# Anew ordering the 1,099 steps of a convolution-and-FFN kernel: other 32-row runs, other places for loads

## The chip, the cores and the metric

One core of a Trainium2 chip runs the whole kernel. The metric is device time in microseconds (us) of one execution. The core has a matrix engine (PE, whose weight loads appear apart as PEld), a vector engine (DVE), a scalar engine for activations (ACT), a fourth engine called POOL, and SP, which does nothing here but issue transfers. Transfers move data between DRAM and the on-chip memory SBUF, 128 partitions wide. PE writes its results into eight banks of a second on-chip memory, PSUM; DVE or ACT must empty a bank before PE can use it again.

## The reference: what is computed

Two branches work on the same layernormed input `xn` (2048 rows, 640 columns, bf16), and are multiplied together:

```python
kv  = shift_conv(k, shift_k) * v                        # 4 taps along the rows
y   = irfft(rfft(kv) * rfft(ssm_k))[:2048] + kv * ssm_D # a convolution as long as the sequence
s   = xn * y
g   = silu(gelu(xn @ w1 + b1) @ w2 + b2)                # FFN, 640 -> 1728 -> 640
out = x + s * g
```

## The kernel before

**The FFN branch.** The rows are worked in four chunks of 512. For a chunk, `xn` is transposed on PE (step `tt`, L488) and copied out of PSUM (`te`); fourteen groups `h` of five matmuls each (L504, the last and narrower one L500) make the hidden layer, each followed by a gelu on ACT (`he`, L516 and L513); eight groups `g` of fourteen matmuls of 320 columns (L537) make the output, each with a silu on ACT (`ge`, L545) and a multiply into `xn` (`gm`, L553) on DVE (suffix `.d`) or POOL (`.p`). The last chunk adds the input on DVE (`ga`, L561) and stores from SP (`gs`, L572).

**The convolution branch** computes Fourier transforms as matmuls in two stages. First the taps run on DVE (`cv`, L630 to L641), and the filter is transposed (`kt` L577, copied by `kc`). First stage: `kf` and `uf` (L588, evacuated by `ke` and `ue`), whose results go to DRAM scratch by POOL's stores (`ks` L603, `us` L614) and come back in another layout by SP's loads (`fl` L646 for the filter, `ml` L694 for the data). Second stage: `ff` and `mu` (L451), products with the filter (`mp`, `mq` on DVE, L717; some inputs are first copied by ACT, `mv`, L711) and the first stage of the inverse, `ma` and `mb` (L451). Here `fe` evacuates `ff`, `me` evacuates the inverse, and `mk` (L700, two loads) makes a copy of the filter's transform with neighbouring partitions swapped. POOL stores (`ms`, L744), SP loads back (`yl`, L751), the second inverse stage `y` runs on PE (L759 and L760), DVE multiplies by `xn` (`yt`, L768), adds the input (`yo`, L773) and POOL stores (`ys`, L777). Evacuations are a copy or cast on ACT (suffix `.a`, L145) or DVE (`.d`, L146).

**The 32-row calls.** The second stage works on blocks of 32 rows. One call of `blocks` issues four matmuls of 32x32 weights by 512 columns:

```python
def blocks(out, m, rhs, turn, form, start=True, stop=True):
    t = int(TURNS[turn])
    ...
    for i in range(P // QB):
        j = (i + t) % (P // QB)
        a, b = (slice(x * QB, (x + 1) * QB) for x in ((i, j) if m == F2 else (j, i)))
        nc.tensor.matmul(out=out[b, :], lhsT=mats[a, m, a], rhs=rhs[a, :], start=start, stop=stop)
```

The digit of `TURNS` for the call's number shifts the four blocks: with turn t, rows i of the array meet columns i+t (forward `ff`, `mu`) or rows i+t meet columns i (inverse `ma`, `mb`). So the sixteen 32x32 tiles of PE's array are used four by four, and two neighbouring calls use the same tile where their turns put them there. There are 160 calls, 640 such matmuls; calls that follow each other on PE without other work between form what is called a run below.

**What sets the order.** A string `PLAN` lists all steps after a fixed opening (`prologue`): a kind, a number and, where there is a choice, an engine or form as a suffix. `steps` (L925 and following) maps a kind to a function. The steps are issued in that order; each engine keeps its own instructions in this order, SP its loads, POOL its stores. PSUM banks and the SBUF slots are handed out by free lists in the same order, so who waits for whose buffer follows from the string too. The first loads of the string are `X` (input chunks, L275), `C` (filter, L305, 512 KB each), `K` (L280 to L282, 640 KB), `V` (L285, 320 KB) and `B` (second FFN weights, L309; the last with two small ones, L311 and L312). Small steps in it: `ls`, `lv`, `lr`, `lb`, `ln` are the layernorm (L458 to L481; `lr` is POOL's power, L467, `lb` is L471), `ir` five POOL instructions (L657 to L660), `s` two on DVE (L417, L418), `q` loads of the input (L748).

Of the kernel before, what the change touches and what calls it, by code (L numbers as in the profile page):

```python
# [38 lines left out]
ke13.a kc12.d gm1.d kf37 kc3.a kf5 kt13 X3 kt15 kc7.d kf3 kf30 ke37.a kf4 kc2.d kf23 ke12.a K1 kc13.d kf31 ke3.a ke4.a
d kt11 kt6 gm0.d kc15.d kt8 ke31.a ke30.d kc11.a kt9 kc6.d kc8.d kc9.a ke5.d kt14 kc14.d kt5 kf34 V1 ke23.a kf35 kf18  # L40
K2 V6 kf26 kc5.d kt0 ke34.a kf14 ke26.a kc0.d ke14.a kf33 kf38 kf45 ke45.a kf43 ke43.a g3 V4 kf15 ke35.a kf36 cv6 ks1
ke33.a kf2 V2 kf22 ke18.a ge3 kf1 ke38.a ke2.a ks11 kf0 ke1.a cv16 kf21 ke0.a g5 ke15.d ke22.a V0 kf44 ke36.a ir ke21.a
cv17 kf46 ge5 gm3.d kf10 ke10.a kf32 kf16 kf17 ke44.a ks12 cv18 ke16.a ks0 kf19 ke32.a cv7 ke19.a ke46.a g7 kf9 kf7
ke17.a ge7 ks10 kf20 ke20.a ks6 kf11 cv19 kf41 cv20 ke7.a kf47 ks4 gm5.d ke47.a kf27 kf28 ks7 g6 ke27.a ks15 uf1 kf40
kf29 ke11.a cv21 ke28.a cv8 kf8 ke9.a ke41.a kf39 ke40.a ke8.a ke39.a ks13 ue1.d uf2 V7 uf7 g4 ke29.a ue2.a ks5 ks9 kf6
X2 ge6 uf4 ge4 cv22 ue7.a kf24 ke6.a V5 kf25 uf9 kf42 h24 uf3 V3 cv23 uf8 ke42.a ke25.a uf0 cv9 ue9.a ke24.a uf6 ue4.a
ue6.a ue8.a cv24 ks3 ue3.a gm7.d h17 ks14 uf5 cv10 uf28 ue5.a cv11 uf11 ue11.a h14 ks2 ue0.a ls9 uf27 h19 h20 he14 ks8
ue27.a uf31 h16 ue31.a ue28.a h18 us2 he17 he19 he24 uf10 h22 ue10.a he16 he22 uf26 uf29 uf30 uf34 ue34.a h23 uf35 h15
# [10 lines left out]
fe30.a fe12.a mk5 ff3.f g11 ff15.q ff16.q ls12 ff17.q fe3.a fe36.d fe33.a ge11 tt10 fe15.d fe16.a ff1.q fe17.a lv3 lr3
mu8.q ff4.q te10.d mu9.f gm11.p fe4.a ff20.q mu7.f mu5.f mq9 fe1.d mv8 mq7 h30 ml5 mv5 h31 h34 mk4 mp9 mu6.q fl15 lb3  # L60
ff25.f ml0 mp5 mp8 mu11.q he30 fe20.d mk1 mu12.q he31 ma9.f ff22.q mp7 mq5 mb9.f mq6 he34 h38 mu10.f fe25.a mv11 me9.a
mp6 ff21.q mk0 fe22.a ma7.f ff37.q fe21.a gm10.p ln12.d mp12 mp10 mb7.f he38 mq10 mu14.q ln13.d mv14 mp11 me7.a fe37.a
h35 h33 ma5.q mu1.q mq12 ln14.d mb5.f ml6 mu0.f he35 ma10.f mu13.q mq1 he33 ff38.q fe38.a me5.a ma6.f mb6.f ml1 mp14
mp1 ml8 mp0 mb10.q h41 me10.a ml12 he41 me6.a h28 mq0 h36 mu3.f he28 ff39.q ml13 mu20.q mu2.q he36 mu4.f mp13 h32 mq13
mk6 ff31.f mk8 mv20 mq3 mk13 mp3 ma3.f mq14 mv2 ma0.f mu15.f fe39.a ml9 mu32.f mb3.f mb0.f ml10 mk9 he32 me0.a mq4
fe31.a mk12 me3.a h29 mp2 h37 mk7 mq15 h39 mv32 ma2.q mq11 he29 mu33.f ma14.q q6 ma12.f mp4 he37 he39 mq2 mb14.q mp15
mp32 mu23.f mq8 mb2.f mb12.f ml15 h40 mp20 mv23 ml14 me2.a mq33 mp33 mu30.q ln15.d me12.a mp23 me14.a mu21.q ma1.q
ma8.q ma11.q mq21 mb1.q mb8.q mb11.q tt16 te16.d mk10 he40 me1.a g17 tt15 mp21 mq20 mu31.q me8.a mp30 mu22.q mq30
mu26.q mp22 ge17 tt19 me11.a ml11 mq31 g18 mp31 te19.a mv26 mu34.q ma31.f te15.a mq22 mq23 ma20.q ma30.q ge18 gm9.p
mp26 ma13.q mb31.f ml7 me31.a q5 ma23.q gm17.p mu25.q mb13.q me13.a mb30.f mp34 mb23.f mq26 me23.a q1 mb20.q me20.a  # L70
mk14 mp25 tt17 g22 mq34 te17.a ma22.q ma32.f mk11 mq32 mu18.q mu16.f ma21.q me30.a mb22.q mb32.q mq25 mb21.q ge22
me21.a me22.a mu17.f q3 mv17 g16 mp18 mq16 me32.a ms3 mu24.q mp16 mq18 ge16 ma4.q gm16.p mu19.q mp17 ma26.q ma34.q
mb4.q mq24 mp19 ma25.q mb34.q ma33.f mb26.q me26.a mp24 me34.a mb25.f me25.a g19 ma24.q mu27.q me4.a mq19 mb24.q mu29.q
# [10 lines left out]
ga26 ys0 g28 yo4.d yt17 yo5.d gs27 ge28 yt22 yt23 gm28.d g25 gm29.d ys5 ge30 ga28 ga29 ge25 gm30.d gm25.d ga25 gs29 g31
ga30 ge31 gm31.d gs25 ys4 gs30 gs31
"""


# [868 lines left out]
```

## Time and profile before

| what | value |
| --- | --- |
| time, median of 3 | 190.81 us (190.59 to 191.03) |
| the profiled execution's own time | 190.82 us |
| its span in the profile | 189.0 us |
| granted PE clock | 0.996 |
| PE busy | 182.8 us, 97% |
| DVE busy | 166.6 us, 88% |
| ACT busy | 158.5 us, 84% |
| POOL busy | 62.3 us, 33% |
| bytes moved | 57.67 MB, mean 305 GB/s |

A row of a timeline has the start and the length in us, the engine, the line of the kernel, the operation, what is written and read, the shape, the number of instructions put together, and in brackets the idle time before them with what ended it. Neighbouring matmuls overlap, so a stretch's length on PE is read from its first start to the start of what follows, and not from the sum of its instructions.

### The profile page before, as it was taken

Reading aid. Unit: us, or ns where it says so; the run is one execution under the profiler, and the core shown is the slowest. Engines: PE = TensorE matmul, PEld = TensorE weight load, DVE = VectorE, ACT = ScalarE, POOL = GpSimd, SP = SyncE. Lnnn points to the kernel's source line nnn. Section 1 sums busy time; section 2 is a strip of 40 time slices with the busy share of each in tenths; the row PEclk is TensorE's granted clock in tenths of the full one; section 3 lists DMA queues with packets and bytes.
Section 4 is the critical chain, followed back from the end, with each engine's and each line's share of the span. In section 5 each row is a group of like instructions: output and inputs, shape, how many; then the busy total and the mean of one; then the engine's idle time right before and its main releaser. Section 6 shows DMA issues by size and latency. Waiting matters only on the chain.

```text
span 189.0 us, 4812 instructions
## 1 busy us (share of the span) xinstructions
PE 182.8 (97%) x1808; PEld 110.2 (58%) x1808; DVE 166.6 (88%) x317; ACT 158.5 (84%) x309; POOL 62.3 (33%) x98
## 2 busy tenths in 40 slices
PE   6899999999999999999999999999999999999992
PEld 2486468977764455665653344465645544677671
DVE  7979899999999999999999999999999600489993
ACT  3757999899999999999999999999898989952021
POOL 8545200029845104157216000030596620010320
PEclk9999999999999999999999999999999999999998
DMA  5999999959899899989789999699799869992545
GB/s 188 376 370 314 347 398 410 358 166 395 329 361 364 287 321 381 297 337 350 236 263 278 341 316 328 229 360 332 234 342 326 317 201 300 394 399 94 212 160 188
DMA packets 26399, 57.67 MB, mean 305 GB/s; under 512 B 3016, under 2 KB 14857, under 8 KB 26376
## 3 DMA queue, kind: packets, MB, share of 16 engines
q1 hardware_dynamic: 21872, 39.65, 61.1%
q0 software_dynamic: 4320, 17.70, 25.4%
q8 instruction: 14, 0.23, 0.5%
q14 instruction: 9, 0.07, 0.1%
q10 hardware_dynamic: 184, 0.01, 0.1%
HBM read 33.76 MB, written 18.35 MB: 276 GB/s over the span
## 4 chain that ended last, share of the span: by engine, by line
PE 85%; DVE 5%; DMA 4%; ACT 3%; issue 1%; SPq 0%; DVEq 0%
PE banks L537 31%; PE banks L504 24%; PE banks L588 9%; PE banks L451 7%; DMA w_sb<-in_B_w_dram 4%; PE banks L832 4%; PE banks L577 3%; PE banks L759 2%; PE banks L760 2%; DVE area L146 2%; PE banks L488 1%; ACT area L145 1%; DVE area L717 1%; PE banks L500 1%; DVE st L458 1%
## 5 line engine op out<-in xcount | busy, mean ns | idle before, releaser
L145 ACT CAST area<-banks 128x512 bf16<-128x512 f32 (+2 forms) x153 | 74.5, 592 | 2.8 <-PE banks L451 1.8
L537 PE MATMUL banks<-w_sb,hT 128*128 128x320 bf16 (+1 forms) x462 | 65.7, 295 | 0.0
L537 PEld LDWEIGHTS <-hT 128*128 128x128 bf16 x462 | 43.7, 98 | 18.1 <-issue 1.9
L504 PE MATMUL banks<-xnT,w_sb 128*128 128x512 bf16 x230 | 53.3, 379 | 0.1
L504 PEld LDWEIGHTS <-w_sb 128*128 128x128 bf16 x230 | 21.7, 98 | 26.7 <-issue 3.5
L516 ACT ACTIVATE hT<-banks,b_f 128x512 bf16<-128x512 f32 x52 | 32.7, 707 | 2.8 <-PE banks L832 1.7
L717 DVE TENSOR_TENSOR area<-banks,area 128x512 bf16<-128x512 f32 x54 | 34.6, 686 | 0.1
L545 ACT ACTIVATE sl<-banks 128x320 bf16<-128x320 f32 (+1 forms) x33 | 14.6, 451 | 14.8 <-PE banks L537 12.9
L553 POOL TENSOR_TENSOR xn<-xn,sl 128x320 bf16<-128x320 bf16 x13 | 10.6, 827 | 48.9 <-ACT sl L545 26.0
L641 DVE TENSOR_TENSOR area<-area 128x2560 bf16<-128x2560 bf16 x16 | 23.5, 1485 | 0.6 <-DMA area<-in_A_k_dram 0.5
L768 DVE TENSOR_TENSOR area<-banks,xn 128x426 bf16<-128x426 f32 (+1 forms) x18 | 10.0, 596 | 14.0 <-PE banks L760 14.0
L451 PE MATMUL banks<-area,mats 32*32 32x512 bf16 x640 | 18.8, 380 | 0.6 <-DVE area L146 0.5
L637 DVE TENSOR_TENSOR area<-area 128x2560 bf16<-128x2560 bf16 x12 | 17.9, 1492 | 0.2
L603 POOL DMA_DIRECT2D scrK<-area x16 | 8.9, 560 | 24.3 <-DVE area L146 18.4
L588 PE MATMUL banks<-area,WB 128*128 128x426 bf16 (+1 forms) x64 | 15.5, 299 | 0.0
L614 POOL DMA_DIRECT2D scrU<-area x16 | 8.7, 547 | 20.6 <-ACT area L145 20.6
L588 PE MATMUL banks<-area,WA 128*128 128x428 bf16 (+1 forms) x64 | 15.4, 298 | 0.0
L146 DVE CAST area<-banks 128x512 bf16<-128x512 f32 (+2 forms) x23 | 14.2, 638 | 0.3 <-ACT area L145 0.2
L451 PEld LDWEIGHTS <-mats 32*32 32x32 bf16 x640 | 6.7, 88 | 10.7 <-issue 8.9
L744 POOL DMA_DIRECT2D scrC<-area x16 | 11.7, 734 | 3.0 <-ACT WB L674 1.4
L717 DVE TENSOR_TENSOR area<-area 128x512 bf16<-128x512 bf16 x26 | 10.5, 420 | 0.0
L458 DVE BATCH_NORM_STATS2 st<-xn 128x6 f32<-128x320 bf16 x24 | 10.4, 476 | 0.0
(109 smaller groups left out, 218.6 us busy)
## 6 DMA issues: line engine op xcount, KB each, us to landing
scrK<-area POOLq DMA_DIRECT2D x16, 320.0 KB, 4.1
scrU<-area POOLq DMA_DIRECT2D x16, 320.0 KB, 3.6
...
```

The lines of the kernel that those rows point to most:

```text
L145: return nc.scalar.copy(out=out_ap, in_=in_ap)
L146: return nc.vector.tensor_copy(out=out_ap, in_=in_ap)
L451: nc.tensor.matmul(out=out[b, :], lhsT=mats[a, m, a], rhs=rhs[a, :], start=start, stop=stop)
L458: nc.vector.bn_stats(out=st[:, j, h, :], in_=xn_tiles[c][:, j, h * HALF:(h + 1) * HALF])
L504: nc.tensor.matmul(out=ps, lhsT=w1_sb[:, t, ft * P:(ft + 1) * P], rhs=xnT[:, t, :], start=(t == 0), stop=(t == DT - 1))
L516: nc.scalar.activation(out=hT[:, ft, :], in_=one(("h", i)), func=ACT.Gelu_apprx_tanh, bias=b1_f[:, ft:ft + 1], scale=1.0)
L537: nc.tensor.matmul(out=ps[:, 0:ws.stop - ws.start], lhsT=hT[0:M, ft, q * P:(q + 1) * P], rhs=w2_sb[0:M, ft, hs.start + ws.start:hs.start + ...
L545: nc.scalar.activation(out=sl[:, ws], in_=one(key)[:, 0:ws.stop - ws.start], func=ACT.Silu)
L588: nc.tensor.matmul(out=ps[:, dst], lhsT=(WA, WB)[r][:, n2, :], rhs=rows[:, n2 % 2, src], start=True, stop=True)
L637: nc.vector.tensor_tensor(out=uc, in0=uc, in1=tmp, op=ALU.add)
L641: nc.vector.tensor_tensor(out=tmp if s else uc, in0=kh[:, r0:r0 + KR, :].rearrange("p (a b) d -> p a b d", a=2), in1=w_exp[:, j:j + 1, Non ...
L717: nc.vector.tensor_tensor(out=p_part(i, x), in0=u, in1=span(name, i), op=ALU.mult)
```

## The change

Two constants change and nothing else: `TURNS` and `PLAN`. The number of steps of each kind and the opening are kept; so is the number of matmuls and of transfers. What moves is the order, and with it some suffixes: filter copies `kc` on DVE 12 to 14, transposes `te` on DVE 10 to 9, `fe` on DVE 11 to 9, `ue` on DVE 8 to 7, `me` on DVE 1 to 3, `ln` on DVE 11 to 12, `gm` on DVE 19 to 20 (each of these goes to or comes from ACT, those of `gm` POOL).

```diff
-TURNS = "303222211332100321313102031211323202233020231231"
+TURNS = "333223311110212303012132122202110030313111121121"
 PLAN = """
-he2 w X1 ls5 h12 h13 h10 C1 ws1 he12 he4 ls6 h9 ls7 he0 he5 ls4 s he10 he9 K0 lv1 B0 lr1 cv1 lb1 ln7.d ln4.d ln6.d he13
...
```

Both orders divide the 160 calls into 22 runs. Calls in each run, in the order of the program:

```
before  2 7 4 6 8 3 7 7 6 10 5 7 8 8 3 12 9 11 6 12 11 8
after   2 7 6 4 3 6 5 6 11 6 10 6 7 3 9 12 9 10 7 13 10 8
```

How often the most used tile of the array is used within each run, worked out from `TURNS` and the order:

```
before  1 2 1 2 4 1 2 3 4 4 2 3 2 3 1 4 3 3 2 5 4 2   sum 58
after   1 2 2 1 1 2 2 3 5 2 5 2 2 1 3 4 3 3 2 4 3 2   sum 55
```

**SP, the loads of the opening.** Before, all of the second FFN weights (L309, L311, L312) stand ahead of the second to fifth filter load (L305):

```order
L305 DMA area<-in_A_ssm_k_dram 128x2048
L280 DMA area<-in_A_k_dram 112x1920
L281 DMA area<-in_A_k_dram 15x1920
L282 DMA area<-in_A_k_dram 128x2560
L309 DMA w_sb<-in_B_w_dram 128x5x640 x2
L309 DMA w_sb<-in_B_w_dram 128x3x640
L311 DMA w_sb<-in_B_w_dram 64x640
L312 DMA w_sb<-in_B_b_dram 1x640
L305 DMA area<-in_A_ssm_k_dram 128x2048 x4
```

The same place on SP in the changed kernel:

```order
L282 DMA area<-in_A_k_dram 128x2560
L309 DMA w_sb<-in_B_w_dram 128x5x640
L305 DMA area<-in_A_ssm_k_dram 128x2048
L309 DMA w_sb<-in_B_w_dram 128x5x640
L309 DMA w_sb<-in_B_w_dram 128x3x640
L311 DMA w_sb<-in_B_w_dram 64x640
L312 DMA w_sb<-in_B_b_dram 1x640
L305 DMA area<-in_A_ssm_k_dram 128x2048 x3
```

One filter load of 512 KB now stands ahead of two of the three large weight loads and the two small ones.

**DVE, the second chunk's layernorm and first transposes** (L641 and L637 are taps and a product of the convolution, L481 the layernorm of a quarter chunk, L146 COPY xnT the first copies of transposes). Before:

```order
L418 TENSOR_SCALAR area<-area 128x384
L463 TENSOR_SCALAR ve_340<-mv_289 128x4
L641 TENSOR_TENSOR area<-area 128x2560
L471 SCALAR_TENSOR_TENSOR nb_346<-mv_289,rs_343 128x4
L481 TENSOR_SCALAR xn<-xn,mv_289,rs_343 128x640 x4
L641 TENSOR_TENSOR area<-area 128x2560
L637 TENSOR_TENSOR area<-area 128x2560
L146 COPY xnT<-banks 128x512
```

In the changed kernel:

```order
L463 TENSOR_SCALAR ve_348<-mv_324 128x4
L641 TENSOR_TENSOR area<-area 128x2560 x2
L417 TENSOR_SCALAR area<-area 128x384
L418 TENSOR_SCALAR area<-area 128x384
L471 SCALAR_TENSOR_TENSOR nb_372<-mv_324,rs_370 128x4
L481 TENSOR_SCALAR xn<-xn,mv_324,rs_370 128x640 x4
L637 TENSOR_TENSOR area<-area 128x2560
L146 COPY xnT<-banks 128x512 x2
```

Two taps and the steps L417 and L418 now stand between L463 and the four L481, where one tap stood before. On POOL the five instructions of `ir`, which stood behind the first two stores of scratch, now stand ahead of the second chunk's L467.

**DVE, the products of the second stage.** L717 are the products, with `banks` where they read PSUM; L146 CAST 128x512 the evacuation of `ff`. Before, from the first product on:

```order
L717 TENSOR_TENSOR area<-banks,area 128x512
L146 CAST area<-banks 128x512
L717 TENSOR_TENSOR area<-banks,area 128x512 x2
L471 SCALAR_TENSOR_TENSOR nb_1480<-mv_1179,rs_1422 128x4
L717 TENSOR_TENSOR area<-area 128x512 x2
L146 CAST area<-banks 128x512
L717 TENSOR_TENSOR area<-banks,area 128x512
L717 TENSOR_TENSOR area<-area 128x512
L717 TENSOR_TENSOR area<-banks,area 128x512 x2
L481 TENSOR_SCALAR xn<-xn,mv_1179,rs_1422 128x640
```

In the changed kernel, from the first product on:

```order
L717 TENSOR_TENSOR area<-banks,area 128x512 x2
L146 CAST area<-banks 128x2x256
L717 TENSOR_TENSOR area<-banks,area 128x512 x3
L471 SCALAR_TENSOR_TENSOR nb_1507<-mv_1216,rs_1505 128x4
L717 TENSOR_TENSOR area<-area 128x512
L717 TENSOR_TENSOR area<-banks,area 128x512
L717 TENSOR_TENSOR area<-area 128x512
L717 TENSOR_TENSOR area<-banks,area 128x512 x4
L481 TENSOR_SCALAR xn<-xn,mv_1216,rs_1505 128x640
L717 TENSOR_TENSOR area<-banks,area 128x512 x7
```

The two evacuations of `ff` that DVE did among its products are one, and it stands ahead of L471; `ff` evacuations behind it are ACT's.

**SP, the reloads of the same stage** (L694 `ml`, L700 `mk`, L748 `q`). Before, from the last filter reload on:

```order
L646 DMA area<-scrK 128x2x640
L694 DMA area<-scrU 128x2x640
L700 DMA area<-area 64x1280 x4
L694 DMA area<-scrU 128x2x640 x5
L700 DMA area<-area 64x1280 x6
L694 DMA area<-scrU 128x2x640 x2
L700 DMA area<-area 64x1280 x6
L748 DMA area<-in_A_q_dram 128x1280
```

In the changed kernel, to the same place (the first L748):

```order
L694 DMA area<-scrU 128x2x640 x2
L700 DMA area<-area 64x1280 x2
L694 DMA area<-scrU 128x2x640 x2
L700 DMA area<-area 64x1280 x4
L694 DMA area<-scrU 128x2x640
L700 DMA area<-area 64x1280 x2
L694 DMA area<-scrU 128x2x640
L700 DMA area<-area 64x1280 x2
L694 DMA area<-scrU 128x2x640
L700 DMA area<-area 64x1280 x2
L748 DMA area<-in_A_q_dram 128x1280
```

The five data reloads that stood together are divided: swapped copies (L700) stand between them, each of which waits until the evacuations that it copies are done. In steps: `ml12 mk6 ml8 ml6 mk10 mk11 ml9 mk8 ml11 mk9 ml10 mk12 q5`, where it was `ml0 mk1 mk0 ml6 ml1 ml8 ml12 ml13 mk6 mk8 mk13 ml9 ml10 mk9 mk12 mk7 q6`. The data reload `ml6` feeds `mu15`, `ml8` feeds `mu20`, and `ml10` feeds `mu26`.

**DVE, the end.** L553 are the last multiplies by the silu, L561 the additions of the input (the last two of each work on 160 columns). Before:

```order
L773 TENSOR_TENSOR area<-area 128x1280
L768 TENSOR_TENSOR xn<-banks,xn 128x426 x2
L553 TENSOR_TENSOR xn<-xn,sl_2731 128x320
L553 TENSOR_TENSOR xn<-xn,sl_2706 128x320
L561 TENSOR_TENSOR xn<-xn,area 128x320 x2
L553 TENSOR_TENSOR xn<-xn,sl_2752 128x320
L553 TENSOR_TENSOR xn<-xn,sl_2756 128x320
L561 TENSOR_TENSOR xn<-xn,area 128x320 x2
L553 TENSOR_TENSOR xn<-xn,sl_2791 128x160
```

In the changed kernel:

```order
L553 TENSOR_TENSOR xn<-xn,sl_2743 128x320
L768 TENSOR_TENSOR area<-banks,xn 128x426
L773 TENSOR_TENSOR area<-area 128x1280
L553 TENSOR_TENSOR xn<-xn,sl_2746 128x320
L553 TENSOR_TENSOR xn<-xn,sl_2750 128x320
L561 TENSOR_TENSOR xn<-xn,area 128x320 x3
L553 TENSOR_TENSOR xn<-xn,sl_2784 128x160
```

A multiply by `xn` (L768) and an addition of 1280 columns (L773) stand nearer to the end, and three L561 in a row stand ahead of the last L553.

More of the change, by code (lines that the diff above doesn't have):

```diff
@@ L39 @@
[L39 to L48, printed above, removed]
@@ L59 @@
[L59 to L68, printed above, removed]
@@ L69 @@
[L69 to L73, printed above, removed]
@@ L84 @@
[L84 to L85 removed]
+he2 X1 C1 w ir h8 he1 h10 he5 K0 B1 ws1 he10 h6 h7 he3 ls7 he0 h13 ls4 ls5 ls6 lv1 C3 h9 B0 cv0 h11 B2 he4 cv1 s lr1
+lb1 he13 ln6.d ln5.d ln4.d ln7.d he8 C0 h12 tt6 he9 tt7 he11 cv2 he6 tt5 te6.d te7.d tt9 tt8 cv3 he7 C2 he12 te5.a
+te9.d ss g0 g1 te8.d ge0 g3 cv4 C4 kt7 gm0.d kt15 sm kt4 cv5 ws0 ws2 d kc7.d kc15.d ge1 V7 ge3 kc4.d kt0 kc0.d kt8 kt9
@@ new lines @@
+uf45 ue38.d uf43 uf46 ls9 uf39 ue36.a us10 g8 ff20.q ue45.a ff35.q ue44.a ue39.d us13 ue43.a ue47.a ue46.a ff5.f us15
+us14 us12 ff7.f gm11.d ls10 ff0.q lv2 ge8 fe35.a ff8.q ff25.f fl1 fe8.a fe5.a g13 ff4.q fe20.a fe7.d lr2 fe0.d ff9.f
+ff11.q ls12 lb2 ln8.d fe25.a ff22.q ff31.q fe9.a gm10.p fe31.a fe4.a ge13 mk3 ff12.f fl13 fe22.a ln11.d fe12.a g9
+ff30.f ge9 ff6.f fe6.a ff28.q ff23.q fl6 fe23.a ls13 gm8.d g14 fe30.a ln10.d ln9.d ml3 fe11.a tt10 tt14 ls15 fe28.d
+tt12 tt13 te10.d ml2 ff2.q ge14 ml5 ff14.q ff10.q tt11 te14.d mk2 ff24.q te12.a fe10.a ff21.f te13.d ff32.q fe2.d
@@ new lines @@
+ff26.q ff18.q te11.d ff34.q g15 ls14 fe14.a mk5 fe21.d fe24.d ff27.f fe26.a gm14.p ff17.f fe32.a fe34.a ml4 fe18.a
+ff3.f ge15 mk4 lv3 gm15.p ff1.f mu9.q h34 h32 he34 fe27.d ff16.q mu14.f ml0 mu5.q fe3.d mu7.q mp9 mq9 fe1.a fe17.d he32
+ff38.f mu6.f h37 fe16.a mq7 h29 ml13 mu8.f mp7 mk0 mk1 ff29.q mv5 mq6 lr3 lb3 mv14 ff15.q mp5 he37 fe38.a he29 ml1 mp6
+mu10.f mq5 mu11.q ma7.f mp10 fe29.a ma5.f mv11 mv8 mu13.q mq10 mb5.q mu12.f mq12 mp12 ml12 fe15.a mb7.f me5.a me7.a
+ln12.d mk6 h40 he40 ma12.q mu0.q mb12.f ml8 mu1.f ff33.q me12.a ff19.q ml6 fe19.a h28 mq13 mk10 he28 h38 mp13 mq0 mp1
@@ new lines @@
+fe33.a ma6.f mk11 mu2.f mu4.f ma10.q mp0 gm9.p he38 mb6.f ma9.q mb9.f mq1 mq4 ln13.d me6.a mp14 ff37.q fe37.a ln15.d
+ln14.d ml9 mp8 mk8 me9.a mb10.f ff39.q mp4 h41 he41 h36 h30 ma0.q mq14 mu32.q mu15.f mq8 mp15 mp11 me10.a fe39.a mu20.f
+mq11 mv2 he36 mb0.f mv20 mp20 mp2 mu3.q mv32 mq3 ml11 mk9 h31 h33 me0.a h39 he31 mp3 ma4.f he30 mu24.f ma13.f mu16.q
+he33 mb4.f ml10 mb13.q ma2.q tt16 mq15 h35 mk12 ms2 he39 gm13.p mq2 mu23.q me4.a mq16 mb2.f q5 me13.a mk13 te16.a he35
+ml7 mp16 mu22.q tt15 g19 ma14.q mq20 mp24 ma11.q me2.a te15.d mk15 mp22 ma8.q mu30.f ml15 mv23 mq24 mu26.q mb14.f mq22
@@ L86 @@
+g30 ga26 yt2 yt23 g28 ge30 gs25 ge28 gm27.d ga27 ge29 gs27 yo0.d gm30.d yt4 g31 ge31 yo1.d gm28.d gm29.d ys0 ys1 ga30
+gs30 ga29 ga28 gs29 gm31.d gs31
 """
```

52 lines of the change are left out of this document (30 added, 22 removed).

## Prediction

> **What bounds the kernel now.** I read the page first: the share of each engine and the chain of waits.
>
> ```profile
> span 189.0 us, 4812 instructions
> PE 182.8 (97%) x1808; PEld 110.2 (58%) x1808; DVE 166.6 (88%) x317; ACT 158.5 (84%) x309; POOL 62.3 (33%) x98
> PE 85%; DVE 5%; DMA 4%; ACT 3%; issue 1%; SPq 0%; DVEq 0%
> ```
>
> PE sets the end: 85% of the chain is its own work, and no matmul is added or removed. An order can only change what PE loses between matmuls. So I read the PE timeline from 76 to 147 us, where the 32-row runs lie. Pieces of it:
>
> ```profile
> 91.74 0.62 PE L451 MATMUL banks<-area,mats 32*32 32x512 bf16 x24
> 92.30 2.08 PE L537 MATMUL banks<-w_sb,hT 128*128 128x320 bf16 x14
> ...
> 98.46 0.42 PE L451 MATMUL banks<-area,mats 32*32 32x512 bf16 x12
> 98.81 0.40 PE L488 MATMUL banks<-ident,xn 128*128 128x128 bf16 x4
> 99.14 0.70 PE L451 MATMUL banks<-area,mats 32*32 32x512 bf16 x16
> 100.01 0.53 PE L451 MATMUL banks<-area,mats 32*32 32x512 bf16 x12 [0.17 <-DVE area L146]
> 100.47 3.41 PE L504 MATMUL banks<-xnT,w_sb 128*128 128x512 bf16 x15
> 103.81 0.61 PE L451 MATMUL banks<-area,mats 32*32 32x512 bf16 x16
> 104.75 0.61 PE L451 MATMUL banks<-area,mats 32*32 32x512 bf16 x12 [0.33 <-DVE area L146]
> ...
> 106.52 1.04 PE L451 MATMUL banks<-area,mats 32*32 32x512 bf16 x24
> 107.50 2.33 PE L504 MATMUL banks<-xnT,w_sb 128*128 128x512 bf16 x10
> ```
>
> Two runs have 24 matmuls, or 6 calls, each. The first takes 92.30 - 91.74 = 0.56 us from its first start to the next work, the second 107.50 - 106.52 = 0.98. In the first the busiest 32x32 tile is used twice, in the second four times. The run of 12 matmuls at 98.46 uses each tile once and takes 98.81 - 98.46 = 0.35. So a run costs about 0.35 plus (0.56 - 0.35) = 0.21 for each further use of one tile ((0.98 - 0.56) / 2 = 0.21 too). What a run costs above that is a wait: at 99.14 the run of 28 (a tile used twice) takes 1.33 instead of 0.56, at 103.81 it takes 1.54 (four times, 0.98 expected). The first start of the second half is late in both, and both name a cast on DVE (L146).
>
> The same reading over all 22 runs gives 18.3 us, against 16.2 if none waited; some 2.1 us are waits. I made both sums from the timeline's L451 rows and their followers; the first is at 77.48, the last at 145.81:
>
> ```profile
> 77.48 0.41 PE L451 MATMUL banks<-area,mats 32*32 32x512 bf16 x8
> ...
> 145.81 0.65 PE L451 MATMUL banks<-area,mats 32*32 32x512 bf16 x32
> ```
>
> **The runs.** Both orders have 22 runs, so what it costs to enter and leave 32-row work is paid as often. The uses of the busiest tile, added over the runs, fall from 58 to 55: 3 x 0.21 = 0.6 us less. The best case is 0.65 and the worst nothing, if it is not the tile that sets a run's length.
>
> Here the Trainium skill ("TensorE: Matmul & The Clock Gate", section "Measured speedup vs the span model") would give another answer: it makes the span of packed tiles one matmul plus about 4 ns for each further tile, which counts tiles and not their repeats. By it the term would be zero. The trace does not agree: two runs of 24 matmuls take 0.56 and 0.98 us. But one of them may hide a wait without a record, so I keep this as a rival.
>
> **The opening.** DVE's and PE's timelines of before:
>
> ```profile
> 19.33 0.17 DVE L463 TENSOR_SCALAR ve<-mv 128x4 f32<-128x4 f32 x1
> 20.03 1.49 DVE L641 TENSOR_TENSOR area<-area 128x2560 bf16<-128x2560 bf16 x1 [0.54 <-DMA area<-in_A_k_dram]
> 21.44 0.15 DVE L471 SCALAR_TENSOR_TENSOR nb<-mv,rs 128x4 f32<-128x4 f32 x1
> 21.52 1.51 DVE L481 TENSOR_SCALAR xn<-xn,mv,rs 128x640 bf16<-128x640 bf16 x4
> ...
> 24.79 0.83 PE L488 MATMUL banks<-ident,xn 128*128 128x128 bf16 x12
> 25.46 3.97 PE L537 MATMUL banks<-w_sb,hT 128*128 128x320 bf16 x28
> ```
>
> Before, DVE waits for a load until 20.03, does one tap, and has the four L481 done at 21.52 + 1.51 = 23.03, well before PE's first L488. Now a second tap (21.44 - 20.03 = 1.41 from start to start) and L417 and L418 come ahead of L471; the two stood inside that wait before:
>
> ```profile
> 18.71 0.31 DVE L417 TENSOR_SCALAR area<-area 128x384 int32<-128x384 f32 x1
> ...
> 19.58 1.05 POOL L467 TENSOR_TENSOR rs<-ve,mhalf 128x4 f32<-128x4 f32 x1 [2.73 <-DVE ve L463]
> 42.59 0.16 POOL L657 IOTA kcol<- 128x1 f32 x1
> ...
> 45.27 2.40 POOL L660 TENSOR_SCALAR kj<-kj,kcol 128x16 int16<-128x16 int16 x1
> ```
>
> L417 and L418 take 19.33 - 18.71 = 0.62. The last L481 ends at 23.03 + 1.41 + 0.62 = 25.06. PE has the same eight `h` groups ahead of its first L488, so its turn comes at 24.8 again; a transpose step takes the four normalised pieces one after another, so only its last waits: 0.1 to 0.4 us. POOL's five `ir` instructions, 45.27 + 2.40 - 42.59 = 5.1 us, now stand ahead of the power (L467) that L471 needs. POOL was free from 19.58 - 2.73 = 16.85, so the power ends at 16.85 + 5.1 + 1.05 = 23.0, and DVE reaches L471 at 21.44 + 1.41 + 0.62 = 23.5. The taps hide it, by 0.5; without them L471 and all behind it would be later by what is missing.
>
> The second FFN weights come next. L311 is the last of them but one (the last row, L312, is 1.2 KB):
>
> ```profile
> 16.94 1.62 SPq L311 DMA_DIRECT2D w_sb<-in_B_w_dram  x1
> DMA to landing us min/median/max: 9.6/9.6/9.6
> DMA packets 2616, 5.69 MB, mean 379 GB/s; under 512 B 162, under 2 KB 1820, under 8 KB 2614
> ```
>
> Before it landed at 16.94 + 9.6 = 26.5, and the first L537 group needed it for its fourteenth matmul. Now 512 KB go ahead, at the 379 GB/s of the stretch from 17 to 32 us 1.4 us: 27.9. But all five transpose steps now stand ahead of that group: it begins at 24.8 + 20 x 0.06 = 26.0 (12 transposes took 25.46 - 24.79 = 0.67), its eleventh to fourteenth matmul run 10 to 13 x 0.138 later, 27.4 to 27.8 (28 matmuls of 320 take 3.97). That loses 0 to 0.4, and less where the transposes were late themselves. I take +0.3 for the opening; bounds 0 and +0.9.
>
> **The waits in the runs.** The two recorded waits come from DVE's casts of `ff` among the products:
>
> ```profile
> 102.67 0.76 DVE L471 SCALAR_TENSOR_TENSOR nb<-mv,rs 128x4 f32<-128x4 f32 x1
> ...
> 104.02 0.68 DVE L146 CAST area<-banks 128x512 bf16<-128x512 f32 x1
> ```
>
> The cast at 104.02 stands behind an L471 of 0.76 us, and the call at 104.75 needs the bank that it empties at 104.70. In the new order DVE's last cast of `ff` stands ahead of L471; the `ff` evacuations behind it are ACT's. So 0.17 + 0.33 = 0.5 us go. What is late next: the banks that the products themselves empty, since DVE stays full (10.00 of 10.00 us):
>
> ```profile
> 100.00:110.00 10.00, 9.66 (x116) 3.82 (x118) 10.00 (x21) 9.60 (x18) 3.29 (x4) 1.00 0.99 314
> L146 DVE COPY area<-banks 128x640 bf16<-128x640 bf16 x12 | 5.4, 485 | 0.4 <-ACT area L145 0.2
> L145 ACT COPY area<-banks 128x640 bf16<-128x640 bf16 x4 | 2.8, 702 | 0.2 <-PE banks L577 0.2
> ```
>
> (Behind the colon: length, then busy us of PE, PEld, DVE, ACT and POOL, the clock, the DMA share, GB/s.) Of the moved suffixes only the two `kc` weigh: +2 x 0.485 = 1.0 us on DVE, -2 x 0.70 = 1.4 on ACT, both long before this stage; the others nearly cancel (`fe` -2 against `me` +2). So I see no relief for DVE beyond the 0.5, and take -0.5. The bounds are -2.1 (all waits go) and +1.6 (rival 1).
>
> **The tail.** PE's work from the first `y` on is the same. DVE's end of before:
>
> ```profile
> 182.19 1.10 DVE L768 TENSOR_TENSOR xn<-banks,xn 128x426 bf16<-128x426 f32 x2
> ...
> 185.21 0.24 DVE L553 TENSOR_TENSOR xn<-xn,sl 128x160 bf16<-128x160 bf16 x1
> ...
> 186.05 0.24 DVE L561 TENSOR_TENSOR xn<-xn,area 128x160 bf16<-128x160 bf16 x1
> ```
>
> From the L768 to the last pieces DVE has 185.21 - 182.19 = 3.0 us of work in a row. In the new order its last multiplies wait for the last silus but one, and behind them stand three L561 of about 0.24 before the last pieces; the last matmuls and the last silu are where they were. That fits in by a hair: +0.1, bounds 0 and +0.3 (one L561).
>
> **The sum**, against the profiled execution's own 190.82 (the median of three is 190.81): -0.6 + 0.3 - 0.5 + 0.1 = -0.7, so 190.1 us.
>
> **Rivals.** *1, slower: the data reloads held up on SP.* `ml6` stands behind `mk6` and `ml8` on SP, and `mk6` waits for the evacuation `fe15`. Before, five data reloads went out together, long before their calls:
>
> ```profile
> 105.32 2.87 SPq L694 DMA_DIRECT2D area<-scrU  x5
> 108.28 5.09 SPq L700 DMA_DIRECT2D area<-area  x6
> DMA to landing us min/median/max: 3.6/5.6/6.9
> ```
>
> After `fe15`, the two loads of `mk6` (5.09 / 6 = 0.85 each), `ml8` and `ml6` (2.87 / 5 = 0.57 each) and 5.6 to 6.9 to landing make 8.4 to 9.7 us. PE's work from there to `mu15`, which needs `ml6`, is five `h` groups of 1.1, one of 0.7, and 19 calls in four runs (2.4 by the price above): 8.6. So `mu15` waits 0 to 1.1 us; `mu26` behind `ml10`, which stands behind two more swapped copies, 0 to 0.5 by the same reckoning. The rival takes the long landings: 1.6 in all, in place of nothing: 190.1 + 1.6 = 191.7. It decides where landings take over some 6 us. For it speaks the DMA share of 0.99; against it, that a landing of 5.6 just fits.
>
> *2, faster: nearly all waits in the runs go.* 190.82 - 0.6 + 0.3 - 1.3 + 0.1 = 189.3: 1.3 of the 2.1 us go in place of 0.5. For it speaks that ACT comes 1.4 us less loaded into the stage and that one late bank makes the next late; against it, that DVE has no slack from 100 to 110 us.
>
> *3, the opening costs its bound of +0.9:* 190.82 - 0.6 + 0.9 - 0.5 + 0.1 = 190.7, or 191.0 where in addition the -0.5 comes to only -0.2. For it speaks that three terms (L481, weights, POOL) point the same way.
>
> *4, the turns do nothing,* a run's length being its count of matmuls (640 in 22 runs in both): then -0.6 falls out, 190.7. The two runs of 24 speak against it.
>
> **Chances.** Forecast 0.45, its own range 189.5 to 190.6; rival 1 0.24 (191.7); rival 2 0.17 (189.3); rival 3 0.08 (191.0); rival 4 0.06 (190.7). A measurement of this kernel can tell some 0.2%, 0.38 us, from no change: faster is below 190.43, slower above 191.19. Of the forecast 0.30 lies below and 0.15 between; rival 2 is faster; rival 3 half between, half above; rival 4 between. Faster 0.30 + 0.17 = 0.47, same 0.15 + 0.04 + 0.06 = 0.25, slower 0.24 + 0.04 = 0.28. The range, 189.2 to 191.9, reaches to rival 2's and rival 1's time and leaves out what lies beyond.
>
> **What the changed profile would show.** The runs: the sum over the 22 runs 0.6 us less where none waits, with a run of 9 calls whose tiles are used three times at most near 0.8, and one of 11 with five uses near 1.2. The opening: the first L537 at 26.0 to 26.4 and no gap inside its first group. The waits: no run cut in two with DVE L146 as releaser after the first products. Rival 1: PE idle with `area<-scrU` as releaser near 110 us. The tail: DVE's last instruction 0.9 us behind the last matmul, as before (186.29 against 185.40). I am wrong if PE's losses appear in the first stage, where the order of `kf` and `uf` changed too and where PE had no gaps before.

## The result, and the profile after

The changed kernel takes 193.42 us (median of 4, 193.37 to 193.89) against 190.74 for the kernel before (190.59 to 191.03): ratio 1.0144, 95% interval 1.0116 to 1.0171. It is 2.7 us slower; 190.1 was forecast, with a range to 191.9.

The page of the changed kernel, the same three rows as were shown of the kernel before (span and instructions, engines, chain of waits):

```profile
span 192.1 us, 4802 instructions
PE 183.4 (95%) x1808; PEld 110.3 (57%) x1808; DVE 169.7 (88%) x319; ACT 157.6 (82%) x308; POOL 57.9 (30%) x97
PE 60%; DVE 24%; ACT 5%; issue 4%; DMA 4%; SPq 0%
```

PE's share of the chain falls from 85% to 60% and DVE's rises from 5% to 24%. The share does not say where time was lost: some 20 of DVE's 46 us in this chain are taps between 45 and 73 us, where the record has a single wait of PE above 0.06 us, of 0.08. The span grew by 192.11 - 189.04 = 3.07 us, somewhat more than the medians, as the profiled execution of the changed kernel was the longest of its four (193.89). From the two PE timelines, by the times at which the same amount of work is done:

| stage | before | changed | lost |
| --- | --- | --- | --- |
| opening, to the first L577 | 31.62 | 31.68 | 0.06 |
| from there to the first `y` (L759) | 129.64 | 130.76 | 1.12 |
| of it, the 22 runs | 18.27 | 18.89 | 0.62 |
| first `y` to the start of the last matmul | 23.91 | 24.24 | 0.33 |
| from there to DVE's end | 1.13 | 1.36 | 0.23 |
| DVE's end to the end of the program | 2.74 | 4.07 | 1.33 |

Nearly half the loss lies behind the last computation. The rest is waiting on PE, and the runs with the greatest part of it are these (PE timeline of the changed kernel):

```profile
105.50 0.72 PE L451 MATMUL banks<-area,mats 32*32 32x512 bf16 x24
106.42 0.88 PE L451 MATMUL banks<-area,mats 32*32 32x512 bf16 x20 [0.20 <-ACT hT L516]
107.38 1.24 PE L504 MATMUL banks<-xnT,w_sb 128*128 128x512 bf16 x5
...
115.78 0.40 PE L451 MATMUL banks<-area,mats 32*32 32x512 bf16 x4
116.41 0.64 PE L451 MATMUL banks<-area,mats 32*32 32x512 bf16 x20 [0.23 <-DVE area L717]
116.98 3.41 PE L504 MATMUL banks<-xnT,w_sb 128*128 128x512 bf16 x15
...
147.15 0.42 PE L451 MATMUL banks<-area,mats 32*32 32x512 bf16 x12
147.96 0.76 PE L451 MATMUL banks<-area,mats 32*32 32x512 bf16 x20 [0.38 <-DVE area L717]
...
178.36 2.06 PE L537 MATMUL banks<-w_sb,hT 128*128 128x320 bf16 x14 [0.17 <-DVE area L768]
```

The run at 115.78 takes 116.98 - 115.78 = 1.20 us where its tiles ask for 0.56 to 0.6 (six calls, two uses of a tile). The run at 147.15 has eight calls with two uses; it takes 1.49 in place of some 0.6. In both PE waits for DVE's products.

**Why DVE is late.** Each DVE instruction can be compared with the usual length of its line and shape (0.15 us for L471); what a row has above that, where it is over 0.1 us, is called its excess here. In the kernel before, two L471 have an excess, 0.90 us in all: 0.61 at 102.67, beside a multiply on POOL (L553), and 0.30 at 89.49, beside the issue of a store on POOL (L614). In the changed kernel it is 3.63, and all of it lies in six instructions, each at a moment in which POOL multiplies. Five of the six are in these rows or the text behind them, the sixth is an L717 of 0.57 at 129.70. DVE, then POOL, of the changed kernel:

```profile
113.54 0.41 DVE L717 TENSOR_TENSOR area<-area 128x512 bf16<-128x512 bf16 x1
113.88 1.54 DVE L481 TENSOR_SCALAR xn<-xn,mv,rs 128x640 bf16<-128x640 bf16 x2
...
143.54 0.90 DVE L670 TENSOR_SCALAR area<-area 128x512 int32<-128x512 int32 x1
144.35 1.01 DVE L717 TENSOR_TENSOR area<-area 128x512 bf16<-128x512 bf16 x1
...
172.90 1.38 DVE L561 TENSOR_TENSOR xn<-xn,area 128x320 bf16<-128x320 bf16 x1
```

```profile
114.07 0.80 POOL L553 TENSOR_TENSOR xn<-xn,sl 128x320 bf16<-128x320 bf16 x1
...
144.15 1.86 POOL L553 TENSOR_TENSOR xn<-xn,sl 128x320 bf16<-128x320 bf16 x2
...
173.28 0.80 POOL L553 TENSOR_TENSOR xn<-xn,sl 128x320 bf16<-128x320 bf16 x1
```

The row at 113.88 holds two L481, of which the first took 1.19 and the second the usual 0.44. An L717 between SBUF operands takes 0.41 at 113.54 and 1.01 at 144.35, beside POOL's multiply; an L561 takes 0.31 elsewhere and 1.38 at 172.90; an L471 at 90.41 took 0.75. The prediction had quoted such a row of the kernel before without seeing it: the L471 of 0.76 at 102.67, which stands beside this on POOL:

```profile
101.13 2.28 POOL L553 TENSOR_TENSOR xn<-xn,sl 128x320 bf16<-128x320 bf16 x3
```

**Why the end is late.** POOL's last long instruction is a drain behind its last store. Of the kernel before, the last stores on POOL's timeline, and the drains of the program's last line (shortest, median and longest in ns, then first and last start):

```profile
182.56 1.07 POOL L777 DMA_DIRECT2D out_dram<-area  x2 [2.65 <-DVE area L773]
```

```profile
L952 POOLq DRAIN  x3: 40/93/5212, 183.1 to 188.8; - x3
L952 SPq DRAIN  x3: 7/7/13, 188.0 to 188.5; - x3
```

Of the changed kernel the same two views:

```profile
186.31 0.54 POOL L777 DMA_DIRECT2D out_dram<-area  x1 [1.06 <-DVE xn L553]
```

```profile
L952 POOLq DRAIN  x3: 40/102/5049, 186.3 to 191.8; - x3
L952 SPq DRAIN  x3: 7/7/7, 189.9 to 191.6; - x3
```

Before, the drain ends at 183.06 + 5.21 = 188.27, a moment after SP's own end at 188.06: the two paths are nearly equal. In the changed kernel SP is done at 189.9, but the drain began at 186.28 and ends at 191.33. The last store that POOL issues has moved from 183.10 to 186.31, and the program's end follows it by 5.9 and 5.8 us. It comes 0.8 us behind the drain's end in both.

### The profile page after: what moved, and what is told of

It is laid out like the page before. It is cut to its first block, busy times and chain, and to the rows that moved or that the text cites. A ratio compares the mean times of both kernels' runs of the same rounds, so it can differ in the third digit from the quotient of the medians.

```text
span 192.1 us, 4802 instructions
## 1 busy us (share of the span) xinstructions
PE 183.4 (95%) x1808; PEld 110.3 (57%) x1808; DVE 169.7 (88%) x319; ACT 157.6 (82%) x308; POOL 57.9 (30%) x97
## 4 chain that ended last, share of the span: by engine, by line
PE 60%; DVE 24%; ACT 5%; issue 4%; DMA 4%; SPq 0%
PE banks L537 21%; PE banks L504 17%; DVE area L641 7%; PE banks L451 7%; DVE area L717 6%; ACT area L145 5%; DMA w_sb<-in_B_w_dram 4%; PE banks L832 4%; PE banks L588 3%; DVE area L637 2%; PE banks L760 2%; PE banks L759 2%; DVE area L768 2%; PE banks L488 2%; PE banks L577 2%
## 5 line engine op out<-in xcount | busy, mean ns | idle before, releaser
L145 ACT CAST area<-banks 128x512 bf16<-128x512 f32 (+2 forms) x154 | 75.9, 605 | 1.6 <-PE banks L451 1.3
L537 PE MATMUL banks<-w_sb,hT 128*128 128x320 bf16 (+1 forms) x462 | 65.6, 296 | 0.2 <-DVE area L768 0.2
L537 PEld LDWEIGHTS <-hT 128*128 128x128 bf16 x462 | 43.4, 98 | 18.9 <-issue 2.9
L516 ACT ACTIVATE hT<-banks,b_f 128x512 bf16<-128x512 f32 x52 | 33.9, 705 | 5.7 <-PE banks L504 3.5
L717 DVE TENSOR_TENSOR area<-banks,area 128x512 bf16<-128x512 f32 x54 | 34.1, 680 | 0.0
L641 DVE TENSOR_TENSOR area<-area 128x2560 bf16<-128x2560 bf16 x16 | 23.5, 1486 | 1.5 <-DMA area<-in_A_k_dram 1.0
L451 PE MATMUL banks<-area,mats 32*32 32x512 bf16 x640 | 19.3, 381 | 1.0 <-DVE area L717 0.6
L768 DVE TENSOR_TENSOR area<-banks,xn 128x426 bf16<-128x426 f32 (+1 forms) x18 | 9.8, 591 | 9.6 <-PE banks L760 9.6
L637 DVE TENSOR_TENSOR area<-area 128x2560 bf16<-128x2560 bf16 x12 | 17.7, 1482 | 0.1
L553 POOL TENSOR_TENSOR xn<-xn,sl 128x320 bf16<-128x320 bf16 x12 | 9.9, 828 | 26.1 <-DMA area<-scrU 13.5
L588 PE MATMUL banks<-area,WB 128*128 128x214 bf16 (+1 forms) x64 | 16.0, 299 | 0.1
L614 POOL DMA_DIRECT2D scrU<-area x16 | 8.6, 543 | 17.2 <-ACT area L145 14.4
L146 DVE CAST area<-banks 128x512 bf16<-128x512 f32 (+2 forms) x22 | 13.4, 635 | 0.4 <-PE banks L451 0.3
L777 POOL DMA_DIRECT2D out_dram<-area x6 | 3.3, 554 | 30.5 <-DVE xn L553 23.6
L717 DVE TENSOR_TENSOR area<-area 128x512 bf16<-128x512 bf16 x26 | 10.9, 442 | 0.0
```

Of the source, the lines that this page charges most:

```text
L145: return nc.scalar.copy(out=out_ap, in_=in_ap)
L146: return nc.vector.tensor_copy(out=out_ap, in_=in_ap)
L516: nc.scalar.activation(out=hT[:, ft, :], in_=one(("h", i)), func=ACT.Gelu_apprx_tanh, bias=b1_f[:, ft:ft + 1], scale=1.0)
L537: nc.tensor.matmul(out=ps[:, 0:ws.stop - ws.start], lhsT=hT[0:M, ft, q * P:(q + 1) * P], rhs=w2_sb[0:M, ft, hs.start + ws.start:hs.start + ...
L588: nc.tensor.matmul(out=ps[:, dst], lhsT=(WA, WB)[r][:, n2, :], rhs=rows[:, n2 % 2, src], start=True, stop=True)
L637: nc.vector.tensor_tensor(out=uc, in0=uc, in1=tmp, op=ALU.add)
```

## The experiments

All times are medians, with the ratio to runs of the kernel before on the same chip. In these later runs the opening varied: the first filter transpose (L577) began between 30.8 and 33.0 us, and in five of the eleven profiles the transposes then waited 0.3 to 0.6 us, in three of them for their load by the record. In the two profiles above they did not. So stages are compared as well as times.

**1. The last store on SP** (`ys1`, changed kernel).

```diff
-        nc.gpsimd.dma_start(out=out_v[...], in_=pair(("o", i)))
+        (nc.sync if i == 1 else nc.gpsimd).dma_start(out=out_v[...], in_=pair(("o", i)))
```

> The changed kernel with one store moved: ys1, the last output store of POOL (issued at 186.31), is issued by SP instead. Theory 'POOL's last store': after POOL's last store begins, POOL's final drain ends 5.0 to 5.2 us later (183.10 to 188.27 before, 186.31 to 191.33 changed) and the program 0.8 us after that; SP was done at 189.93 in the changed kernel and 188.06 before. With ys0 (184.70) as POOL's last store the drain ends at 189.8 and SP sets the end, about 1.0 us after 189.93: span 190.9 against 192.1, time 1.2 us less (192.2). Rival 'last landing': the end follows the last bytes to land (189.78); the store lands no sooner from SP, so the span stays at 192.1 within 0.3.

193.89 us, ratio 1.0144 (1.0092 to 1.0196): no gain in time, in a profile whose first `y` was 1.5 us later than in the changed kernel's. From the last matmul's start to the end it took 4.78 us instead of 5.43. POOL's drain was over at 191.16 and was no longer last, but SP's end then came at 192.03, 2.4 us behind its last issue (1.8 in the changed kernel), as it had the 320 KB of `ys1` to finish too (drains of this kernel):

```profile
L952 POOLq DRAIN  x3: 40/102/4967, 186.2 to 192.7; - x3
L952 SPq DRAIN  x3: 7/7/117, 192.0 to 192.4; - x3
```

So half of the 1.2 came, and the other half was lost to a second path. Alone this run does not tell the theories apart.

**2. One addition late, in the kernel before.** The opposite edit: the same work, with POOL's last store delayed.

```diff
-... g28 yo4.d yt17 yo5.d ... g31 ga30 ge31 gm31.d gs25 ys4 ...
+... g28 yt17 yo5.d ... g31 ga30 ge31 yo4.d gm31.d gs25 ys4 ...
```

> The kernel before with one addition moved: yo4 (0.73 us on DVE) stands right ahead of the last multiply gm31, so that the store ys4, POOL's last, is issued at about 185.8 instead of 183.10. All other work is as before. Theory 'POOL's last store': the drain ends at 185.8 + 5.2 = 191.0, the span at 191.7: 2.6 us slower. Rival 'last landing': the 320 KB land some 2.5 to 2.9 us after issue, at 188.6, where SP was done at 188.06 before: 0.5 to 0.8 us slower.

193.78 us, ratio 1.0161 (1.0111 to 1.0212): 3.1 us slower by moving one DVE instruction of 0.73 us. The store was issued at 186.64, later than worked out, as `yo4` ran at 185.52 (POOL's timeline, and the drains of this kernel):

```profile
186.64 0.54 POOL L777 DMA_DIRECT2D out_dram<-area  x1 [3.56 <-DVE xn L553]
```

```profile
L952 POOLq DRAIN  x3: 40/93/5049, 186.6 to 192.2; - x3
L952 SPq DRAIN  x3: 7/7/7, 190.0 to 191.9; - x3
```

SP was done at 190.0, the drain at 186.62 + 5.05 = 191.67, and the end came at 192.43, again 0.8 behind the drain. The last bytes of the program had landed at 189.33, 3.1 us ahead of the end; in the kernel before they landed 1.1 us ahead of it (187.90). So the end follows POOL's drain and not the landings: over all profiles of this study the drain lasts 4.97 to 5.23 us from the last store on. Not all of the 3.4 us by which this span is longer is the drain's: some 0.7 arose between the first L577 and the first `y`, and SP's own path was 2.0 us later too. With an end 1.0 us behind SP's, as in the kernel before, it alone would have ended the program at some 191.0.

**3. Four multiplies from POOL to DVE** (changed kernel).

```diff
-gm13.p ... gm22.p ... gm21.p ... gm17.p
+gm13.d ... gm22.d ... gm21.d ... gm17.d
```

> The changed kernel with four multiplies moved from POOL to DVE: gm13, gm17, gm21, gm22. Theory 'DVE held by POOL': DVE instructions that overlap these four POOL multiplies took 0.75, 1.06 and 0.47 + 0.59 us longer than their like (L481 at 113.88, L561 at 172.90, L670 at 143.54, L717 at 144.35); DVE gives 4 x 0.23 for doing them itself and wins 2.9 - 0.9 = 1.9, and the PE waits that name DVE behind them (0.6 at 115.78, 0.9 at 147.15, 0.3 at 177.85) go for the most part: time 1.0 to 1.7 us less than 193.4. Rival 'DVE is just full': the long rows are chance, and four more instructions on a full DVE make it 0 to 0.6 us slower.

192.37 us, ratio 1.0072 (1.0031 to 1.0114): 1.0 us less than the changed kernel, though DVE has four instructions more. (The spans of the two profiles differ by 2.1, as this one is of an execution shorter than its median, 191.81.) DVE's excess falls from 3.63 to 0.75, and the two late runs have lost their waits (PE timeline of this kernel):

```profile
115.63 0.65 PE L451 MATMUL banks<-area,mats 32*32 32x512 bf16 x24
116.22 3.41 PE L504 MATMUL banks<-xnT,w_sb 128*128 128x512 bf16 x15
...
146.62 0.84 PE L451 MATMUL banks<-area,mats 32*32 32x512 bf16 x32
147.40 2.08 PE L537 MATMUL banks<-w_sb,hT 128*128 128x320 bf16 x14
```

1.20 has become 0.59, 1.49 has become 0.78, the wait at 178 is gone, and the 22 runs take 17.85 in place of 18.89. The first `y` comes at 161.18, the last matmul starts at 185.09, both a little earlier than in the kernel before. What is left is the end: POOL's last store at 184.24, the end at 190.03.

**4. The four multiplies and the end's order.** As 3, and the last additions and stores ahead of the last multiplies:

```diff
-yt23 g28 ge30 gs25 ge28 gm27.d ga27 ge29 gs27 yo0.d gm30.d yt4 g31 ge31 yo1.d gm28.d gm29.d ys0 ys1 ga30
+yt23 yt4 yo0.d ys0 yo1.d ys1 g28 ge30 gs25 ge28 gm27.d ga27 ge29 gs27 gm30.d g31 ge31 gm28.d gm29.d ga30
```

> The changed kernel with the four multiplies gm13, gm17, gm21, gm22 on DVE and, at the end, yt4, yo0, ys0, yo1, ys1 moved ahead of g28's, gm27's and gm30's steps, so that POOL's last store is issued some 1.2 us earlier; same work. With the four multiplies alone the profile had POOL's last store at 184.24, its drain to 189.26, SP done at 188.00 and the end at 190.03. Theory 'POOL's last store': the store at 183.0, drain to 188.1, SP sets the end at 188.0 + 1.0: span 189.0, 1.0 us less than with the multiplies alone. Rival 'last landing': SP's last store is where it was, so no gain.

191.03 us, ratio 1.0034 (1.0005 to 1.0062); span 189.13, 0.9 less than with the four multiplies alone and 0.1 from the kernel before. POOL's last store came at 183.17, the drain ended at 188.36, SP was done at 187.87. SP's last store was issued 0.1 us earlier than in 3, so the gain is not from the last landing. By the medians these two edits together take back 2.4 of the 2.7 us, by the ratios 2.1.

**5. And two more.** As 4, with `gm10` on DVE and the tap `cv0` behind the four L481, as it stood in the kernel before.

```diff
-B0 cv0 h11 ... ln7.d he8 ... gm10.p
+B0 h11 ... ln7.d cv0 he8 ... gm10.d
```

> The one with four multiplies and the end moved, and besides gm10 on DVE too (L471 at 90.2 was held 0.44 us by it) and the tap cv0 behind the four L481 of the second chunk, as in the kernel before. Theory: the transposes of the opening lose their 0.2 us wait, DVE wins 0.44 - 0.23 = 0.2: 0.2 to 0.4 us less than without these two, and 0.2 to 0.6 less than the kernel before, since the runs without waits are 0.55 shorter. Rival 'what PE wins becomes waits for DVE and ACT': no difference that the timing shows.

191.27 us, ratio 1.0051 (1.0032 to 1.007): no gain. In its profile the filter transposes lost 0.33 us, where the record names DVE's L687, which stands behind a tap of 1.48, and `uf14` waited 0.43 for DVE, which 4 had as 0.30; the 22 runs were as in 4 (17.80 and 17.81). The L471 at 91.17 took 0.16 in place of 0.75, and nothing came of it.

**6. The multiplies left on POOL, at other places.** As 4, but `gm13`, `gm21`, `gm22` stay on POOL and only change place in its order; `gm17` and `gm10` on DVE.

```diff
-gm9.p ... ms2 ... gm13.p ... gm20.p ... ms1 ... gm22.p ... gm21.p
+gm9.p gm13.p ... ms2 ... gm20.p gm22.p ... ms1 gm21.p
```

> The changed kernel with three multiplies kept on POOL but at other places of POOL's order, where DVE works on PSUM: gm13 behind gm9, gm22 behind gm20, gm21 behind ms1; gm17 and gm10 on DVE; the end ordered as in the kernel with four multiplies on DVE and the end moved. Over all profiles so far a DVE instruction with an operand in PSUM that overlapped a POOL multiply was never longer than its like by more than 12 ns, one between SBUF operands alone often by 150 to 1,060 ns. Theory 'what DVE does at that moment decides': holds of DVE stay under 0.6 in all (3.47 in the changed kernel), though POOL still does the three; the sum of the 22 runs is 17.2 to 17.8 us, PE's waits at 115.8 and 147.2 are gone, span 188.5 to 189.2. Rival 'POOL's load itself costs DVE': holds come back with the three multiplies, 1 us and more, runs 18.3 or more.

190.98 us, ratio 1.002 (0.9993 to 1.0048). DVE's excess is 0.30 (the 3.47 of the expectation counts 0.44 for the L471 at 90.41 of the changed kernel, in place of 0.60), the 22 runs take 17.29, 1.6 less than in the changed kernel, and the span is 188.93. So it is not POOL's load that costs DVE: the same three multiplies cost nothing where DVE reads PSUM. The rival falls. This profile lost 0.48 us at the filter loads and 0.64 at `uf14`; together 0.8 more than in 4, which is more than the runs gained on 4 (0.5). The times of 4 and 6 do not differ by more than their noise.

**7. The same cause in the kernel before.** `gm9` and `gm13` on DVE; then `gm9` and `gm18`.

```diff
-gm13.p ... gm9.p ... gm18.p
+gm13.d ... gm9.d ... gm18.p    (first)
+gm13.p ... gm9.d ... gm18.d    (second)
```

> The kernel before with gm9 and gm13 on DVE in place of POOL: L471 at 102.67 was held 0.46 us by gm9 and the cast behind it was awaited by PE (0.33 recorded, 0.54 over the run's length without waits). Theory 'DVE held by POOL': that run falls from 1.54 to 1.0 to 1.2 us and the time by 0.2 to 0.5. Rival: DVE is full and two more instructions cost it 0.47; nothing or slower by up to 0.4.

> The kernel before with gm9 and gm18 on DVE. With gm9 and gm13 on DVE the run at 104 fell from 1.54 to 0.80 us, but gm18 came to hold an L717 for 0.62 us, and the run behind it grew from 1.24 to 1.72. With gm18 off POOL too: runs 0.7 shorter than in the kernel before (17.5 to 17.7), time 0.4 to 0.8 us less. Rival 'the holds only move': another POOL multiply meets an SBUF instruction of DVE, and the time is within 0.3 us of before.

The first: 191.07 us, ratio 1.002 (0.9995 to 1.0045). The run at 104 fell from 1.54 to 0.80 as expected, but the gain was gone 35 us later: DVE was a little earlier, and an L717 between SBUF operands now met `gm18` (timelines of POOL, DVE and PE of the first):

```profile
138.88 0.80 POOL L553 TENSOR_TENSOR xn<-xn,sl 128x320 bf16<-128x320 bf16 x1
```

```profile
138.95 1.03 DVE L717 TENSOR_TENSOR area<-area 128x512 bf16<-128x512 bf16 x1
```

```profile
139.45 1.79 PE L451 MATMUL banks<-area,mats 32*32 32x512 bf16 x48
141.17 1.25 PE L504 MATMUL banks<-xnT,w_sb 128*128 128x512 bf16 x4
```

That run of twelve calls took 1.72 where it had taken 1.24. The second: 190.54 us, ratio 0.9993 (0.997 to 1.0016), span 188.74; the runs take 18.02, 0.25 less than before (0.7 was expected), and some 0.6 was lost at the filter loads. No version beat the kernel before by more than the measurement tells.

**8. The turns.** Three kernels. With other digits in `TURNS` alone, the kernel before, where the uses of the busiest tile fall from 58 to 54; the same with `gm9` and `gm13` on DVE; and the kernel of 6 with digits by which the uses rise from 55 to 81.

```diff
-TURNS = "303222211332100321313102031211323202233020231231"
+TURNS = "103322213112100123030012010213132232013022312131"
```

```diff
-TURNS = "333223311110212303012132122202110030313111121121"
+TURNS = "333222211332112321313132131211323232233120231231"
```

> The kernel before with other digits in TURNS and nothing else changed; the 22 runs keep their calls. The lengths that the runs would have without waits (0.35 us plus 0.21 for each further use of a tile, worked out call by call) fall from 16.17 to 15.37. Theory 'tile repeats count': runs that did not wait shorten by their share, the sum of the 22 runs falls by 0.3 to 0.8 us (part may turn into waits for DVE and ACT) and the time by the same. Rival 'only the number of matmuls counts': each run keeps its length, time within 0.2 us of before.

> The kernel before with the other TURNS (lengths of the runs without waits 15.37 in place of 16.17) and gm9 and gm13 on DVE, so that no POOL multiply holds a DVE instruction in that stage, which had confused the run with other TURNS alone (a new hold of 0.64 at 89.95, sum of the runs 18.82 instead of 18.27). Theory 'tile repeats count': the sum of the 22 runs is 0.4 to 0.8 us less than with gm9 and gm13 on DVE and the old TURNS, and so is the time. Rival 'PE's gain becomes waits': less than 0.2 of the 0.8 arrive.

> The kernel with gm13, gm21, gm22 at other places of POOL's order, gm17 and gm10 on DVE and the end moved, with other digits in TURNS and nothing else changed: the uses of the busiest tile, added over the 22 runs, rise from 55 to 81. Theory 'tile repeats set a run's length': 26 x 0.21 = 5.5 us more in the 22 runs, less what stands in a run as a wait already: run by run the longer of the old measured length and the new length without waits, 22.7 us in all against 17.3; time 4 to 5.5 us more. Rival 'only the number of matmuls counts': the runs stay at 17.3 and the time within 0.5 us. Between them, 'DVE and ACT set the pace of the stage': single runs grow as the theory says, but they shift to the next waits, and less than half arrives.

The first took 190.76 us, ratio 1.0008 (0.9974 to 1.0041); its 22 runs grew from 18.27 to 18.82, with a new hold of DVE by POOL (0.64 at L481, 89.95). The second took 191.05, ratio 1.0025 (0.9993 to 1.0058); beside the first kernel of 7 its runs took 18.55 instead of 18.41. None of the 0.8 us that the tiles would give arrived. But the second was no clean test either: its run at 105.49 waited 0.38 us for a filter reload (`scrK`), for which the first kernel of 7 did not wait, and in both of them `gm18` held an L717 by 0.62. The third took 195.38, ratio 1.0243 (1.0195 to 1.0291): 4.4 us more than 6. Its runs took 21.46 instead of 17.29, 4.2 of 5.5 us. A run of seven calls that waits for nothing shows the tile at work, with two uses in 6 (first) and five in this kernel (second; PE timelines):

```profile
136.37 0.64 PE L451 MATMUL banks<-area,mats 32*32 32x512 bf16 x28
136.94 0.40 PE L488 MATMUL banks<-ident,xn 128*128 128x128 bf16 x4
```

```profile
139.64 1.26 PE L451 MATMUL banks<-area,mats 32*32 32x512 bf16 x28
140.83 0.40 PE L488 MATMUL banks<-ident,xn 128*128 128x128 bf16 x4
```

0.57 against 1.19 us for the same 28 matmuls: 0.62 for three further uses, 0.21 each. So a repeat costs what was worked out, and of a bad choice of turns some three quarters are paid. A better choice than the kernel's gained nothing in two trials, each with a new wait of its own; that DVE and ACT set the pace of the stage would explain it, but is not shown.

## Why the prediction was wrong, by its steps

**The runs, -0.6.** The price holds (0.21 for a further use; runs without a wait come out as worked out, 0.37 for four calls, 0.76 for nine with three uses). Added up by that price alone, the 22 runs of the kernel before need 22 x 0.35 + 36 x 0.21 = 15.3 us, not the 16.2 of the prediction, which the expectations of 8 call worked out call by call; so the waits in them are 2.1 to 3.0 us. The difference of three uses is the same either way. What fell is that the sum arrives: the 22 runs took 0.62 more. Whether the 55 uses gain anything by themselves stays open: with most of the holds removed in both, the changed order's runs take 17.29 (6) and the old order's 18.02 (second of 7), but the orders differ in more than their turns, and in 8 a fall of four uses gained nothing, beside new waits. Rival 4 (the turns do nothing) is excluded by the third kernel of 8.

**The opening, +0.3.** The first L537 group began at 25.95 without a gap, as forecast. The transposes lost 0.1 us; the stage to the first L577 lost 0.06, or 0.2 if one counts that this profile's beginning was 0.14 earlier. The term was right within 0.3. One of its inputs was wrong and did no harm, which is luck: the five `ir` instructions, put at 5.1 us, took 18.25 - 16.66 = 1.6. In the kernel before, their two long ones (L660) took 2.00 us at 43.06 and 2.40 at 45.27, while DVE worked on taps between SBUF operands (L641, L637, L630); in the changed kernel the same two took 0.61 at 17.11 and 0.33 at 17.92, while DVE worked on statistics (L458). All profiles of the old order have the first two values, all of the new order the last two. This points to POOL being held beside DVE as well; no run was made to test it, and that row too was read as a price.

**The waits in the runs, -0.5.** This step failed. The two waits for DVE's casts went, as forecast, and no run is cut by L146. But the step asked only which instruction DVE does ahead of the awaited one, and took its length from the rows. It did not ask what POOL does at the same moment. The order moved `gm13`, `gm21`, `gm22` and `gm17` to where DVE works between SBUF operands, and DVE lost 2.9 us in four instructions; PE lost 1.0 us of it in the runs and 0.33 in the `y` stage (3). The L471 of 0.76 us in the prediction was the same thing: a row five times as long as its like was read as a price, not as a question. The rest of the wait in the stage, at 105.5 to 108.8 (recorded for ACT in the changed kernel) and at 72 for DVE's tap, some 1.1 us, is in nearly all variants of the new order; its cause was not traced further and stays open.

**The tail, +0.1.** This step failed by 1.5 us, of which 1.33 behind DVE's end. The prediction began with the premise that an order can only change what PE loses between matmuls, and this stretch lies behind the last of them. The term followed DVE and the last silus, and priced an L561 at 0.24; it did not follow POOL's last store, which waits for `yo1`. That store came 3.2 us later in the new order, and POOL's drain of 5.05 us behind that store became the last path. The rows for it, the store at 182.56 and the drain to 188.3, equal with SP's end, were in the profile of before.

**Rival 1** (reloads late on SP) did not occur: of PE's waits in the changed kernel, none names a data reload, and the run with `mu15` and `mu20` waited for DVE's L717 (waits of PE, changed kernel: us in total, times, longest).

```profile
PE banks L832 <- DMA w_sb<-in_B_w_dram: 0.6, 1, 0.6
PE banks L451 <- DVE area L717: 0.6, 2, 0.4
...
PE banks L451 <- ACT hT L516: 0.2, 1, 0.2
```

The slower outcome that I had given a chance of 0.28 came, by two ways that stood in none of the rivals.
